# Attention and MLP mixer on one core: the first half of the first queries loaded by GpSimd with a cast, instead of by SyncE and cast on ScalarE

## The chip, the cores and the metric

The kernel runs on one core of a Trainium2 chip. The metric is the time of one execution in microseconds, as the device gives it. Times of several executions are given as a median with the lowest and the highest.

## The reference

Blockwise causal attention, followed by a mixer over tokens and channels. Eight batches, eight heads, 576 tokens, 64 channels per head; all inputs and the output are float32.

```python
scores = scale * np.matmul(q, k.transpose(0, 1, 3, 2))
mask = block_i >= block_j                      # blocks of 64 tokens
scores = np.where(mask, scores, -1000000000.0)
attn = np.exp(scores - np.max(scores, axis=-1, keepdims=True))
attn = attn / (np.sum(attn, axis=-1, keepdims=True) + 1e-09)
x = (attn @ v)                                 # heads side by side: B, 576, 512
h = np.maximum(x.transpose(0, 2, 1) @ w_tok1, 0.0) @ w_tok2
u = x + h.transpose(0, 2, 1)
out = u + np.maximum(u @ w_ch1, 0.0) @ w_ch2
```

## The kernel before

Every piece of work (a load, a cast, a set of matmuls, an evacuation, a store) is an operation with a number. `ORDER` is a written-out list of these numbers, each with the engine that does it (T TensorE, A ScalarE, D VectorE, P GpSimd, S SyncE) and, in small letters, the PSUM banks that it takes. The program is issued in that order, and each engine works through its own share of it strictly in sequence. The order is thus fixed by hand, not by a scheduler at run time, and an operation that waits holds up all that follows on its engine.

A batch goes through these stages: k and q of four heads (a head group, two per batch) are loaded and brought to bf16 in `qk_sb`; VectorE transposes them in blocks of 32 (line 442); TensorE makes the scores of four heads (line 566), ScalarE exponentiates them into `e_sb` (line 585 for batch 0, line 772 for the others); TensorE multiplies with v (`vals`, line 616; line 669 for the last 64 tokens); VectorE normalises into `x_sb`. Then come the token mixer and the channel mixer, whose matmuls fill most of the kernel; the next batches' attention runs between them.

Batch 0 has no work to hide behind, so its loads are cut up. In `load_qk` each of k and q is loaded in two halves of 9 of the 18 rows per partition; q of head group 0 has three pieces, 9, 5 and 4 rows. The first three pieces, both halves of k and the first of q, are loaded by SyncE as float32 into a staging area that lies in `gT` (line 425) and cast to bf16 by VectorE or ScalarE (lines 402 and 400). The other pieces are loaded by GpSimd, which casts on the way (line 437). All loads of v (line 468), of the weights (479, 502, 511) and of later batches' k and q (418) also go through GpSimd's queue. A DMA issued by GpSimd occupies GpSimd while it is issued.

While TensorE has nothing else to do in the first microseconds, it runs matmuls on zeros (lines 371 and 378).

A batch's 512 output rows that this part handles are stored by `channel_down_fast` from the `o_sb` buffers: the upper half (`row == 0`) as one DMA for each 128 rows, the lower half as one DMA for 256 (line 1455). Most stores go through SyncE, where DMA transposes for the channel mixer (lines 969 and 979) stand between them.

Of the kernel before, what the change touches and what calls it, by code (L numbers as in the profile page):

```python
# [27 lines left out]
class Plan:  # L28
# [72 lines left out]
    13S 22P 24P 5P 9D 2D 3P 16S 44Ta 12P 19S 10P 4P 30P 14D 15D 17A 32P 1D 26P 18D 20A 28P 0A 45Tb 23D 25D 21D 252P 46Tb  # L101
    47Tb 48Tb 49Ta 50Ta 37P 51Ta 52Ta 53Ta 54Ta 55Ta 56Ta 35P 57Ta 7D 174Tst 175T 34P 195A 58Ta 59Ta 60Ta
    61Ta 196A 62Ta 38P 197D 63Ta 31D 64Ta 65Ta 66Ta 176A 199Tt 36P 177A 178D 67Ta 179D 68Ta 33D 69Ta 255P 70Ta 200A
    180Ts 27D 198P 71Ta 72Ta 40P 73Ta 181A 29D 182Tt 157P 74Ta 75Ta 76Ta 183A 77Ta 201Ts 43P 78Ta 79Ta 80Ta 253D
    202A 42P 214Tt 254D 188Tb 189T 41P 215A 184Tc 11D 233Ts 6D 190D 191D 258P 192Td 211Ta 234A 220Tt 216P 256D 39P
    185T 257D 221A 81Tb 218Ts 155P 212D 213D 207Tb 235D 208T 186D 219A 158P 187D 237Tt 193D 209D 156P 203Ta 210D
    204T 238A 194D 239Ts 261P 205D 206D 164P 8D 240A 236D 269Tcbda 424P 271A 163P 281Tefgh 270A 166P 259D 273A 217D
    226Tb 283A 227T 284A 222Tc 223T 228D 241Ta 242T 282A 229D 165P 249Tf 224D 245Tg 285A 225D 162P 246T 230Tb 243D
    244D 339Tc 159P 250D 231D 232D 337Ta 251D 247D 161P 340A 260D 272A 276Tbfeh 338D 348Tc 262D 160P 278A 349T 263D
    345Ta 280A 346T 248D 277A 341Td 350D 421P 301Tgbfh 274D 347D 264P 343Tc 342D 303A 275D 351Ta 304A 265P 352T 344D  # L110
    305A 425D 354Td 355T 302A 313Tcbfh 279A 356D 306P 387Tg 353A 267P 426D 384Td 315A 388T 266P 316A 404Ta 385T 317A
    268P 408Tb 314A 381Te 386D 405A 416Tf 427P 409D 390Tc 389A 307P 391T 333D 430P 372Td 392A 308Tabhg 167P 373T
# [12 lines left out]
    553T 623A 763D 543T 620A 547D 676Tg 621A 761D 544A 644Tdehf 542D 926P 677A 554D 555T 647A 764D 560Tag 648A 556D
    561Tc 929P 563A 680Th 557D 765P 562A 684Tf 681D 645A 566T 558T 685D 646A 564Tc 567A 649D 559D 651Tdhef 650P 565A
    768P 638Ta 653A 635Tb 772P 639D 568T 652A 640D 570T 636D 654A 637D 686Ta 569D 655A 656Tbdhe 571D 641Tc 660A 687D
    629Tf 659A 573T 642D 630D 689S 643D 632Ta 658A 631D 682Te 572D 657A 788Tcfdh 633D 634D 574A 673Tb 683D 790A
    670Ta 674D 789A 664Tg 688S 675D 671D 579Tef 672D 791A 665D 792A 666D 769D 783Tbagc 580A 667Td 784A 661Th 668D
    581T 785A 669D 662D 786A 663D 767D 787A 776Tdhba 582D 842Tc 779A 766D 778A 575D 932P 840Tb 780A 941P 770D 777A  # L130
    583Ta 930D 773P 841A 576D 843A 781P 820Tdgeh 939P 577D 585T 771P 821A 578D 824A 775P 584D 694Tbc 850Td 774P 690D
    697A 587T 586D 822A 935P 691D 823A 782P 692D 698Th 851D 848Tg 588D 699A 700T 849D 695Td 701A 704T 696D 702T 589T
    705D 703D 693D 808Tabde 931D 707T 590D 810A 844Tg 812A 846Th 845D 809A 793Tb 591T 708A 847D 811A 794D 795D 813P
    815Tacde 592D 814P 805Tb 1024P 819A 802Tg 594S 806D 818A 799Th 807D 854S 803D 724Tfe 817A 800D 709Tdb 801D 816A
    727D 710Tc 712A 725Th 927D 711A 728Ta 855S 928D 726A 715T 804D 796Tc 729A 934D 730T 716A 713Th 933D 731A 734T
    420S 797D 798D 714A 732T 593S 735D 943Tcgdf 733D 719T 945A 736D 717T 946A 720D 831Ta 944A 834Tg 718D 737T 947A
    722T 835D 836D 738A 828Td 948P 832D 833D 950Tgchf 723A 829D 830D 837Ta 721D 953A 852Tb 838D 952A 839D 857D 825Td
    951A 853D 876Tea 1036P 954A 877Tc 858D 856S 879A 826D 861Tbh 827D 1035P 878A 862Tg 859D 864D 891Tfd 949P 863A
    880Tc 940P 706D 894A 882T 739D 881A 942P 865Tg 897T 937D 866A 938P 867T 936D 883A 884T 860D 1021P 868A 871T 885D
    1030P 869T 898A 886T 872D 1027P 987Tbcef 870D 874T 887D 1034P 990A 895Tg 988A 875D 889T 991A 1007Te 740D 989A  # L140
    896A 890D 955Tbchf 741D 892Ta 959A 899T 1026D 956A 901T 893D 958A 1009Tf 957A 1008D 902D 975Tbach 1010D 972Te
    978A 904T 900D 979A 960Tf 1025D 969Tc 905A 743Tgh 961D 976A 973D 1122P 974D 962D 977A 970D 971D 982Tefdb 980D
    744A 981D 1022D 966Ta 984A 963Tc 1023D 745T 985A 967D 888D 1119P 986A 964D 965D 983A 1037P 995Td 968D 873A 998Tc
    746D 1050Tabfe 1033P 996D 999D 992Tg 1000D 1054A 749T 993D 1053A 994D 997D 1052A 1028D 1038Tcdge 1051A 1029D
    1004Tb 1041A 1031D 1001Ta 1125P 1040A 747Tf 1032D 1039A 1002D 1003D 1128P 1005D 1006D 1082Tdcga 1135P 748D
    1017Tb 1084A 742D 751T 1083A 1018D 1086A 750D 1042A 1045Tcdba 1085A 752D 1043P 753T 1047A 1131P 1121D 757S 1049A
    1120D 1044P 1048A 1077Tdegf 754D 1064Ta 1080A 1124D 1061Tb 755T 1046A 1065D 1062D 1063D 1079A 1078A 1070Tbcge
    1081A 756D 1067Td 1074A 1123D 1058Tf 1073A 1104Th 1066D 1059D 1071A 1060D 1130D 1072A 1055Ta 1143Tfbeg 1105A
    1056D 1075P 1057D 1015Tc 1134P 1068D 1146A 1127D 1013Ta 1145A 1069D 1102Th 1129D 1147A 1076D 1144A 1014D 1093Td
    1103A 1090Tb 1016D 1136Taegf 1126D 1020S 1099Tc 1137A 1094D 1114Th 1091D 1092D 1140A 1100D 1087Ta 1101D 1139A  # L150
    903D 1096Tb 1088D 1112Tc 1138A 1089D 758S 1108Tf 1095D 1115A 1141P 1113D 1106Ta 1132P 1175Tdgeh 1097D 1142D
    1098D 1011Tc 1133P 1107D 1179A 1336Tb 1177A 1012D 1178A 1109D 1168Tachg 1176A 1110Te 1116S 1171A 910Tdf 1170A
    1111D 1337A 1169A 1334Tc 1117S 911D 906D 1148Tbahe 912T 907D 1150A 1019S 1172A 1151A 916T 1173P 913D 1152A 1174P
    1149A 908D 1118S 1180Tadgh 909D 1153Tb 1183A 914Te 1154D 1184A 1155D 1181A 917D 1194Tb 1182A 1335D 1159Tg 1191Th
    1195D 1185Ta 1196D 1197Td 1160D 1192D 1165Tb 1193D 920T 915D 1161D 1198D 1199D 1166D 1188Th 1167D 921D 1162Td
    1156Tb 1189D 1249Tcg 1190D 918T 1163D 1164D 1252A 1200D 1201D 922T 1186D 919D 1157D 1255T 1158D 924S 1279Ted
    1187D 923D 1280Tb 1282A 1350Ta 1256A 1281A 1234Tch 1351A 1344Tf 1237A 1283Tb 1345D 1285T 1284A 1240T 1286A
    1338Ta 1241A 1250Tf 1339D 1253Te 1251A 1287T 1202D 1254A 1348Tc 1288D 1203D 1259T 1349A 1257T 1238Ta 1258D 1289T
    1239A 1235Tb 1290D 1342Tc 1236A 1244T 1291D 1343D 1356Tf 1242T 1245D 1219Tbc 1243D 1360Te 1260D 1220Ta 1361A
    1357D 1262T 1222A 1292T 1364S 1263D 1221A 1340Te 1247T 1293D 1223Ta 1341D 1358Td 1224A 1246D 1204Tfg 1359D 1248A  # L160
    1205Te 1225T 1207D 1206A 1264Tdh 1226A 1229T 1479D 1267A 1265Te 1230D 1208Tb 1266A 1227T 1480D 1209D 1270T
# [1403 lines left out]
```

## Time and profile before

| | |
|---|---|
| median of 3 runs | 284.88 us (284.14 to 289.33) |
| profiled execution | 284.84 us, of it a span of 283.1 us from the first to the last instruction |
| TensorE busy | 276.5 us, 98% of the span |
| VectorE busy | 239.1 us, 84% |
| ScalarE busy | 179.3 us, 63% |
| GpSimd busy | 72.4 us, 26% |
| DMA | 31.97 MB in 64891 packets; software queue (GpSimd) 53.8%, hardware queue (SyncE) 19.7% of 16 engines' time |

In the profile's lines PE is TensorE, PEld its weight loads, DVE VectorE, ACT ScalarE, POOL GpSimd and SPq SyncE's queue. "out<-in" names the tiles written and read; L442 is line 442 of the kernel. The chain is followed back from the last instruction, at each step to what released it.

### The profile page before, as it was taken

The numbers are of one execution on the slowest core, as the hardware profiler recorded it, in microseconds if no ns is written. First come the engines' busy times: TensorE is split into PE (matmuls) and PEld (weight loads), VectorE is DVE, ScalarE is ACT, GpSimd is POOL, SyncE is SP. The second block draws the span as 40 slices with busy tenths as digits, with TensorE's granted clock in tenths as the row PEclk, the third lists the DMA queues.
The fourth block names the chain that finished last, engine by engine and source line by source line (L and its number), as shares of the span: only waits on it lengthen the run. The fifth ranks groups of instructions, "written<-read, shape, count | busy, mean of one in ns | idle before, by whom it ended". The sixth has DMA issues, their size and how long they took to land.

```text
span 283.1 us, 9609 instructions
## 1 busy us (share of the span) xinstructions
PE 276.5 (98%) x4110; PEld 204.7 (72%) x4110; DVE 239.1 (84%) x515; ACT 179.3 (63%) x331; POOL 72.4 (26%) x126
## 2 busy tenths in 40 slices
PE   8999999999999999999999999999999999999995
PEld 3566656588776788986877658756789876568884
DVE  4578669999889898999998979959897897579984
ACT  3798788953998856897779866274533744652200
POOL 8885760511631351063232221000000000000000
PEclk9999999999999999999999999999999999999999
DMA  7999999955989792999698595100044502100157
GB/s 174 161 181 198 198 195 200 140 89 113 109 97 135 81 153 55 165 194 166 72 117 144 43 195 67 59 21 19 0 78 91 206 0 76 74 2 2 74 151 223
DMA packets 64891, 31.97 MB, mean 113 GB/s; under 512 B 53200, under 2 KB 55888, under 8 KB 64848
## 3 DMA queue, kind: packets, MB, share of 16 engines
q0 software_dynamic: 44896, 17.49, 53.8%
q1 hardware_dynamic: 19520, 13.21, 19.7%
q8 instruction: 32, 0.52, 0.8%
q10 hardware_dynamic: 432, 0.66, 0.7%
q14 instruction: 11, 0.09, 0.1%
HBM read 35.85 MB, written 9.44 MB: 160 GB/s over the span
## 4 chain that ended last, share of the span: by engine, by line
PE 90%; POOL 3%; ACT 3%; DMA 2%; issue 1%; DVE 0%; POOLq 0%
PE late L1364 23%; PE mm L1103 8%; PE mm L1230 7%; PE mm L566 7%; PE mm L1364 7%; PE late L1230 6%; PE late L1103 6%; PE mm L616 5%; PE mm L807 3%; PE mm L902 2%; PE late L616 2%; PE late L902 2%; PE late L566 2%; DMA vals<-in_v_dram 2%; PE late L1030 2%; PE mm L1030 2%
## 5 line engine op out<-in xcount | busy, mean ns | idle before, releaser
L772 ACT ACTIVATE e_sb<-mm 128x512 bf16<-128x512 f32 x82 | 46.5, 606 | 13.2 <-PE late L566 9.5
L772 ACT ACTIVATE e_sb<-late 128x512 bf16<-128x512 f32 x86 | 48.4, 609 | 9.2 <-PE late L566 8.4
L442 DVE STREAM_TRANSPOSE qk_sb<-qk_sb 128x288 int32<-128x288 int32 (+1 forms) x65 | 41.7, 693 | 3.8 <-PE late L566 1.8
L468 POOL DMA_DIRECT2D vals<-in_v_dram x45 | 36.9, 832 | 4.7 <-PE mm L616 2.4
L1364 PEld LDWEIGHTS <-gT 128*128 128x128 bf16 x336 | 32.0, 98 | 5.6 <-issue 0.4
L1364 PEld LDWEIGHTS <-sums 128*128 128x128 bf16 x324 | 31.3, 98 | 5.2 <-issue 0.4
L566 PEld LDWEIGHTS <-qk_sb 32*64 32x64 bf16 x1280 | 19.6, 104 | 13.1 <-issue 9.2
L566 PE MATMUL mm<-qk_sb 32*64 32x512 bf16 (+7 forms) x560 | 27.4, 289 | 0.1
L566 PE MATMUL late<-qk_sb 32*64 32x512 bf16 (+7 forms) x560 | 26.8, 295 | 0.6 <-ACT e_sb L585 0.3
L616 PEld LDWEIGHTS <-e_sb 128*128 128x128 bf16 x640 | 23.2, 97 | 5.4 <-issue 2.3
L1364 PE MATMUL late<-wd_sb,gT 128*128 128x256 bf16 x168 | 20.7, 273 | 0.0
L1364 PE MATMUL late<-wd_sb,sums 128*128 128x256 bf16 x168 | 20.6, 273 | 0.0
L1103 PEld LDWEIGHTS <-ws_sb 128*128 128x128 bf16 x192 | 18.2, 98 | 3.0 <-issue 0.9
L616 PE MATMUL mm<-vals,e_sb 128*128 128x65 bf16 x450 | 19.9, 193 | 0.1
L642 DVE TENSOR_TENSOR x_sb<-mm,rinv 128x256 bf16<-128x256 f32 x45 | 18.7, 421 | 1.3
L1410 DVE TENSOR_TENSOR o_sb<-late,u_sb 128x512 f32<-128x512 f32 x22 | 14.9, 683 | 3.6 <-PE late L1364 3.6
L1230 PEld LDWEIGHTS <-ws_sb 128*128 128x128 bf16 x120 | 11.6, 98 | 8.6 <-issue 0.2
L1103 PEld LDWEIGHTS <-wc_sb 128*128 128x128 bf16 x144 | 15.3, 114 | 1.4 <-issue 0.4
L1364 PE MATMUL late<-wc_sb,gT 128*128 128x256 bf16 x132 | 16.2, 272 | 0.0
L594 POOL COPY vals<-e_sb 128x256 bf16<-128x256 bf16 (+1 forms) x11 | 4.3, 392 | 40.6 <-ACT e_sb L772 40.4
L400 ACT COPY mm<-late 128x512 f32<-128x512 f32 (+1 forms) x16 | 9.1, 571 | 8.1 <-PE late L1230 5.3
L793 ACT ACTIVATE gT<-mm 128x512 bf16<-128x512 f32 x21 | 12.6, 616 | 1.9 <-PE mm L1103 0.9
(198 smaller groups left out, 631.8 us busy)
## 6 DMA issues: line engine op xcount, KB each, us to landing
out_dram<-o_sb SPq DMA_DIRECT2D x19, 256.0 KB, 2.4
qk_sb<-in_k_dram POOLq DMA_DIRECT2D x14, 288.0 KB, 6.2
qk_sb<-in_q_dram POOLq DMA_DIRECT2D x14, 288.0 KB, 5.9
vals<-in_v_dram POOLq DMA_DIRECT2D x28, 128.0 KB, 4.8
out_dram<-o_sb SPq DMA_DIRECT2D x7, 512.0 KB, 3.5
wc_sb<-in_moe_w_ch_dram POOLq DMA_DIRECT2D x8, 192.0 KB, 7.0
wc_sb<-in_moe_w_ch_dram POOLq DMA_DIRECT2D x3, 512.0 KB, 10.5
vals<-in_v_dram POOLq DMA_DIRECT2D x15, 64.0 KB, 5.4
```

What stands on the lines that cost most here:

```text
L442: nc.vector.transpose(dst[:, 0:S, :] .rearrange("p s e -> p (s e)") .bitcast(I32) .rearrange("p (a k) -> p k a", k=NB)[:, k0:k1], raw2.bit ...
L468: nc.gpsimd.dma_start(out=t[128 - p : 128, J, hs, 0:64], in_=src)
L566: nc.tensor.matmul(out=home(n)[64 * half : 64 * half + 64, c : c + w], lhsT=bar[r, 0] if j is None else kT[i][r, 64 * j : 64 * j + 64, par ...
L616: nc.tensor.matmul(out=u[:, I, 0:65], lhsT=e[:, h, c : c + 128], rhs=vt[:, J, head, 0:65], start=(J == 0), stop=(J == I),)
L642: nc.vector.tensor_tensor(out=xt[:, 0:4, 64 * head : 64 * head + 64], in0=u[:, :, 0:64], in1=ri[:, 0:4].to_broadcast([128, 4, 64]), op=MULT,)
L772: nc.scalar.activation(dst, bank_of(x), EXP, scale=scale)
L793: nc.scalar.activation(dst, src, RELU)
L902: nc.tensor.matmul(out=bank_of(bank), lhsT=w2_sb[:, t, 128 * si : 128 * si + 128], rhs=at[:, t, :], start=(t == 0), stop=(t == NDT - 1),)
L1103: nc.tensor.matmul(out=bank_of(bank)[:, 256 * o_ : 256 * o_ + 256], lhsT=x(o_, m), rhs=y[:, :, m, :], start=opens, stop=m == 1, skip_group ...
L1230: nc.tensor.matmul(out=bank_of(bank)[:, 128 * c : 128 * (c + step)], lhsT=x(m), rhs=y[:, c : c + step, m, :], start=opens, stop=m == 1, sk ...
L1364: nc.tensor.matmul(out=bank_of(bank)[:, 256 * i : 256 * i + 256], lhsT=x[:, kk, 128 * i : 128 * i + 128], rhs=y[:, kk], start=first and i ...
L1410: nc.vector.tensor_tensor(out=dst, in0=src, in1=other, op=ADD)
```

## The change

The first piece of q of batch 0, head group 0 (9 of 18 rows) is no longer loaded by SyncE into the staging area and cast on ScalarE; it is loaded by GpSimd, cast on the way, as the first DMA of GpSimd's queue. Its transpose on VectorE now comes first of the three of q instead of last. One operation falls away, so all later numbers in `ORDER` go down by one; the sequence of the others on every engine is unchanged. And the store of the lower half of batch 0's rows goes out as two DMAs of 128 rows instead of one of 256. It is the first of the stores that SyncE issues at 118.60 us.

```diff
 ORDER = """
-    13S 22P 24P 5P 9D 2D 3P 16S 44Ta 12P 19S 10P 4P 30P 14D 15D 17A 32P 1D 26P 18D 20A 28P 0A 45Tb 23D 25D 21D 252P 46Tb
+    13S 19P 21P 23P 5P 9D 2D 3P 16S 43Ta 12P 10P 4P 29P 14D 15D 17A 31P 1D 25P 18D 27P 0A 44Tb 20D 22D 24D 251P 45Tb
...
-                if first and not hg and n + f < 2:
+                if first and not hg and n == 0:
                     def emit_load(o, k0=k0, k1=k1, hbm=hbm, n=n):
                         nc.sync.dma_start(out=stage[n][:, D * k0 : D * k1], in_=hbm[:, D * k0 : D * k1])
...
                 def emit(o, row=row, cols=slice(256 * h0, 256 * h1), c0=c0, nt=nt):
-                    step = 1 if row == 0 else nt
+                    step = 1 if row == 0 or b == 0 else nt
                     for t0 in range(c0, c0 + nt, step):
```

In the upper line of `ORDER`, 19S, 20A and 21D are the load, the cast and the transpose of the piece in question, 22P to 25D loads and transposes of the other two pieces of q. In the lower line 19P and 20D are its load and transpose.

More of the change, by code (lines that the diff above doesn't have):

```diff
@@ L176 @@
[L176 to L178 removed]
+    13S 19P 21P 23P 5P 9D 2D 3P 16S 43Ta 12P 10P 4P 29P 14D 15D 17A 31P 1D 25P 18D 27P 0A 44Tb 20D 22D 24D 251P 45Tb
+    46Tb 47Tb 48Ta 49Ta 36P 50Ta 51Ta 52Ta 53Ta 54Ta 55Ta 34P 56Ta 7D 173Tst 174T 33P 194A 57Ta 58Ta 59Ta 60Ta 195A 61Ta
@@ new lines @@
+    240Ta 241T 281A 228D 164P 248Tf 223D 244Tg 284A 224D 161P 245T 229Tb 242D 243D 338Tc 158P 249D 230D 231D 336Ta 250D
+    246D 160P 339A 259D 271A 275Tbfeh 337D 347Tc 261D 159P 277A 348T 262D 344Ta 279A 345T 247D 276A 340Td 349D 420P
+    300Tgbfh 273D 346D 263P 342Tc 341D 302A 274D 350Ta 303A 264P 351T 343D 304A 424D 353Td 354T 301A 312Tcbfh 278A 355D
+    305P 386Tg 352A 266P 425D 383Td 314A 387T 265P 315A 403Ta 384T 316A 267P 407Tb 313A 380Te 385D 404A 415Tf 426P 408D
+    389Tc 388A 306P 390T 332D 429P 371Td 391A 307Tabhg 166P 372T 310A 333D 381T 167P 309A 368Tc 308A 369T 168P 416A
@@ new lines @@
+    1052A 993D 996D 1051A 1027D 1037Tcdge 1050A 1028D 1003Tb 1040A 1030D 1000Ta 1124P 1039A 746Tf 1031D 1038A 1001D
+    1002D 1127P 1004D 1005D 1081Tdcga 1134P 747D 1016Tb 1083A 741D 750T 1082A 1017D 1085A 749D 1041A 1044Tcdba 1084A
+    751D 1042P 752T 1046A 1130P 1120D 756S 1048A 1119D 1043P 1047A 1076Tdegf 753D 1063Ta 1079A 1123D 1060Tb 754T 1045A
+    1064D 1061D 1062D 1078A 1077A 1069Tbcge 1080A 755D 1066Td 1073A 1122D 1057Tf 1072A 1103Th 1065D 1058D 1070A 1059D
+    1129D 1071A 1054Ta 1142Tfbeg 1104A 1055D 1074P 1056D 1014Tc 1133P 1067D 1145A 1126D 1012Ta 1144A 1068D 1101Th 1128D
@@ new lines @@
+    1146A 1075D 1143A 1013D 1092Td 1102A 1089Tb 1015D 1135Taegf 1125D 1019S 1098Tc 1136A 1093D 1113Th 1090D 1091D 1139A
+    1099D 1086Ta 1100D 1138A 902D 1095Tb 1087D 1111Tc 1137A 1088D 757S 1107Tf 1094D 1114A 1140P 1112D 1105Ta 1131P
+    1174Tdgeh 1096D 1141D 1097D 1010Tc 1132P 1106D 1178A 1335Tb 1176A 1011D 1177A 1108D 1167Tachg 1175A 1109Te 1115S
+    1170A 909Tdf 1169A 1110D 1336A 1168A 1333Tc 1116S 910D 905D 1147Tbahe 911T 906D 1149A 1018S 1171A 1150A 915T 1172P
+    912D 1151A 1173P 1148A 907D 1117S 1179Tadgh 908D 1152Tb 1182A 913Te 1153D 1183A 1154D 1180A 916D 1193Tb 1181A 1334D
@@ new lines @@
+    1442A 1328D 1384Te 1386A 1402Td 1399Tc 1385A 1329T 1403A 1400A 1408T 1330D 1406T 1389T 1332S 1407D 1368Tcg 1390A
+    1443Tef 1409D 1371A 1387Td 1411T 1388A 1374T 1412D 1446A 1372Ta 1393T 1524D 1373A 1375D 1369Th 1449T 1394D 1370A
+    1447Tc 1425D 1391T 1448A 1444Th 1392D 1450A 1378T 1445A 1453T 1494D 1379D 1451T 1395A 1376T 1454D 1381T 1396T 1456T
+    1397A 1531Tde 1457D 1382A 1458D 1462Tbh 1459D 1466Tg 1460D 1463A 1461D 1468T 1532D 1527D 1464T 1467D 1535Tf 1465D
+    1452D 1470T 1528D 1455A 1469D 1537T 1529D 1377D 1472T 1471D 1380A 1410D 1476S 1533T 1530D 1473D 1573Tbc 1569D
```

130 lines of the change are left out of this document (53 added, 77 removed).

## The prediction

> **What bounds the kernel now.** I read the page first (busy shares, then the chain that ended last), then the chain in order of time for the first 45 us, because the change acts there.
>
> ```profile
> span 283.1 us, 9609 instructions
> PE 276.5 (98%) x4110; PEld 204.7 (72%) x4110; DVE 239.1 (84%) x515; ACT 179.3 (63%) x331; POOL 72.4 (26%) x126
> PE 90%; POOL 3%; ACT 3%; DMA 2%; issue 1%; DVE 0%; POOLq 0%
> ```
>
> TensorE is busy for 98% of the span and holds 90% of the chain. The other tenth lies at the start. In order of time the chain there reads:
>
> ```profile
> 1.26 1.24 POOL qk_sb L437 x2
> ...
> 6.92 2.78 POOL vals L468 x4
> 9.70 5.39 DMA vals<-in_v_dram
> ...
> 15.13 0.40 PE mm L616 x8
> 15.53 0.63 PE sc L566 x14
> ...
> 16.18 4.99 ACT e_sb L585 x5
> ...
> 21.22 0.66 PE late L566 x14
> ```
>
> The columns are start, length and what ran. The chain does not pass through the first scores. It passes down GpSimd's queue: two q loads, the small fills, six more q and k loads, four v loads, then the fifth v load issued at 9.70, which lands 5.39 later. That landing lets TensorE do value products at 15.13, the scores queued behind them at 15.53, and so ScalarE's exponentials from 16.18. From there ScalarE sets the pace for 4.99 us, and then TensorE. The view by windows says what follows leaves nothing to catch up with:
>
> ```profile
> 22.00:60.00 38.00, 37.39 (x703) 24.37 (x703) 31.90 (x74) 32.81 (x67) 19.16 (x32) 1.00 1.32 184
> 60.00:120.00 60.00, 60.00 (x1087) 48.08 (x1084) 55.56 (x128) 44.03 (x87) 17.45 (x29) 1.00 0.93 107
> ```
>
> The first number in front of a bracket is TensorE's busy time: 37.39 of 38, then 60 of 60. A microsecond gained or lost at 16.18 is one at the end.
>
> **What feeds the first scores.** They wait for five transposes on VectorE, two of k and three of q (timeline, start and length; a bracket is the wait before):
>
> ```profile
> 1.66 0.43 SPq L425 DMA_DIRECT2D gT<-in_q_dram  x1
> 4.47 0.72 DVE L442 STREAM_TRANSPOSE qk_sb<-qk_sb 128x288 int32<-128x288 int32 x1
> 5.19 0.71 DVE L442 STREAM_TRANSPOSE qk_sb<-qk_sb 128x288 int32<-128x288 int32 x1
> 6.37 1.59 DVE L442 STREAM_TRANSPOSE qk_sb<-qk_sb 128x160 int32<-128x160 int32 x3 [0.47 <-DMA qk_sb<-in_q_dram]
> 6.55 0.67 ACT L400 CAST qk_sb<-gT 128x576 bf16<-128x576 f32 x1 [1.39 <-DMA gT<-in_q_dram]
> 8.02 0.51 PE L566 MATMUL sc<-qk_sb 32*64 32x192 bf16 x28 [0.60 <-DVE qk_sb L442]
> 8.78 7.13 ACT L585 ACTIVATE e_sb<-sc 128x384 bf16<-128x384 f32 x9 [1.45 <-PE sc L566]
> 16.18 4.98 ACT L585 ACTIVATE e_sb<-sc 128x1024 bf16<-128x1024 f32 x5 [0.28 <-PE sc L566]
> ```
>
> VectorE is free from 5.90 and waits until 6.37 for GpSimd's first q load; the three q transposes end at 7.96 and the scores start at 8.02. Nine exponentials run from 8.78 to 15.91, then ScalarE idles 0.28 us for the scores that the v load held back. An earlier first exponential therefore only lengthens that 0.28.
>
> **Part 1: what goes.** The cast of 0.67 us stands on ScalarE between idle times of 1.39 and 1.45 us, so its removal is worth 0. SyncE's third issue, 0.43 us, has nothing behind it on SyncE until a store at 66: 0.
>
> **Part 2: the added issue on GpSimd.** The load of the q half goes to the head of GpSimd's queue, ahead of everything that the chain passes through.
>
> ```profile
> L437 POOL DMA_DIRECT2D qk_sb<-in_q_dram x4: 538/550/689, 1.3 to 4.8; - x4
> DMA to landing us min/median/max: 4.1/4.7/5.1
> 4.24 1.08 POOL L437 DMA_DIRECT2D qk_sb<-in_q_dram  x2
> 5.31 1.08 POOL L437 DMA_DIRECT2D qk_sb<-in_k_dram  x2
> 6.35 0.57 POOL L418 DMA_DIRECT2D qk_sb<-in_k_dram  x1
> 6.87 3.65 POOL L468 DMA_DIRECT2D vals<-in_v_dram  x5
> ```
>
> An issue of this kind holds GpSimd 0.54 to 0.69 us, 0.55 in the middle. GpSimd never waits between 1.26 and the end of these rows, so nothing swallows it: all of the queue moves by 0.55, two q loads, the fills, four loads of the second head group, one of the next batch, five of v. The fifth v issue goes from 9.70 to 10.25.
>
> **Part 3: does the landing move as much as the issue?** At most it moves by the issue (0.69 for the longest). At least by 0, if the DMA engines have a backlog that the issue only joins later. The windows of half a microsecond decide (second-last column: share of the DMA engines; last: GB/s):
>
> ```profile
> 5.00:5.50 0.50, 0.50 (x3) 0.20 (x2) 0.50 (x3) 0.15 (x1) 0.50 (x2) 1.00 0.83 153
> 5.50:6.00 0.50, 0.50 (x4) 0.24 (x3) 0.40 (x1) 0.00 (x0) 0.50 (x2) 1.00 0.95 87
> 6.00:6.50 0.50, 0.50 (x7) 0.45 (x6) 0.13 (x1) 0.00 (x0) 0.50 (x2) 1.00 0.95 151
> 6.50:7.00 0.50, 0.50 (x7) 0.46 (x5) 0.50 (x2) 0.45 (x1) 0.50 (x2) 1.00 1.16 175
> ```
>
> From 6.5 on the engines are more than full, so there is a backlog. But between 5 and 6.5 they are not, and move as little as 87 GB/s: the first group's q is nearly in, and the second group's loads, issued from 4.24, have hardly begun. In the new kernel these are issued from 4.79, while the bytes of the first group are the same, so that thin stretch grows and the backlog behind it starts later, by nearly the whole 0.55. I take 0.5 of 0 to 0.69. Behind the fifth v landing (15.09) everything moves by 0.5: ScalarE's second run from 16.18 to 16.68. The last v load of that batch lands near 22 on the same queue and has the same shift, so it is not added.
>
> **Part 4: the first scores.** The new load is first in GpSimd's queue and takes the 4.1 to 5.1 us of the rows of its kind. They hold at most its own size, 144 KB as landed, so I take the upper one, which the first load of the queue had:
>
> ```profile
> gT<-in_q_dram SPq DMA_DIRECT2D x1, 288.0 KB, 4.9
> qk_sb<-in_q_dram POOLq DMA_DIRECT2D x1, 80.0 KB, 5.1
> qk_sb<-in_q_dram POOLq DMA_DIRECT2D x1, 64.0 KB, 4.8
> ```
>
> 1.26 + 5.1 = 6.36, and the transposes, now in the order of the loads, run 6.36 to 7.95 if the other two pieces (issued 1.81 and 2.36) land by 7.1 and 7.5; 2.36 + 4.8 = 7.16 does. So the first scores start as before: 0. The wait for this piece now stands ahead of the other two q transposes on VectorE; TensorE's first scores wait for all three either way, so only the last end counts. Early end: all land 4.1 after issue, VectorE starts at 5.90 and ends at 7.49, 0.47 earlier, which lengthens ScalarE's idle and brings nothing. Late end: a landing of 6.6 us, the longest beside these, among all loads of q and k in the first 20 us:
>
> ```profile
> DMA to landing us min/median/max: 4.1/5.1/6.6
> ```
>
> 1.26 + 6.6 = 7.86, so 1.49 later; that is the second rival.
>
> The fit of the Trainium skill for a load by GpSimd (DMA: Bandwidth & Descriptors, Anatomy of one DMA — SWDGE (gpsimd) path: about 2.0 us plus the bytes at 436 GB/s) would give 2.7 us for the 288 KB read, an estimate by that page; all three pieces would be in before 5.90, which is the early end, with the same end time. The trace has 4.8 to 5.1 us for smaller pieces, so here the measurement decides against it.
>
> **Part 5: the split store.** Batch 0's lower rows leave SyncE as two stores, after two transposes by DMA:
>
> ```profile
> 111.36 0.41 SPq L1455 DMA_DIRECT2D out_dram<-o_sb  x1
> 118.60 2.19 SPq L1455 DMA_DIRECT2D out_dram<-o_sb  x3
> 122.96 1.20 SPq L979 DMA_TRANSPOSE umT<-um_sb  x1
> ```
>
> One more issue costs 0.41. The stores end at 120.79 and the next transpose, which waits for its data, starts at 122.96: 2.17 us cover it. Without that cover it would be 0.41 on the transposed mean rows, whose readers lie far off the chain. 0.
>
> **Sum.** 0 + 0 + 0.5 + 0 + 0 = +0.5 us. The profiled execution took 284.84 us (span 283.1 and 1.74 around it), which is the median of the runs, 284.88, to within 0.04. So 284.84 + 0.5 = 285.3 us.
>
> **The rivals.**
> 1. *The shift is swallowed; not slower.* The backlog after 6.5 us hides the later issue, the v loads land at 15.09 as before. For it: the shares above 1. Against it: the thin stretch just before. Price 0, and if the v data even gain a little from an emptier hardware queue, at most ScalarE's 0.28: 284.6 to 284.8.
> 2. *The q half lands late; slower.* The place is VectorE's first q transpose, now waiting for a longer load through GpSimd. It decides once the nine exponentials, ending at 15.91 plus its delay, end after 16.68, a delay of 0.77, that is a landing 5.9 us after issue. At 6.6 us the delay is 1.49, the exponentials end at 17.40, 1.22 later than 16.18: 286.1. For it: this piece is 1.8 times the longest of the first two. Against it: loads of 144 KB took 4.1 to 5.1.
> 3. *TensorE slows down in the pause; slower.* The trace shows two speeds of the same idle-filling matmuls:
>
> ```profile
> 1.20 4.80 PE L371 MATMUL mm<-wd_sb 128*128 128x512 bf16 x11 [1.20 <-DVE wd_sb L344]
> 5.83 1.58 PE L378 MATMUL mm<-wd_sb 128*128 128x256 bf16 x13
> ```
>
> 0.436 us for 512 columns at first, 0.122 for 256 later, 1.8 times slower per column. The pause before the first scores, 0.60 now, would be 2.1 in the late case, and one before 15.13 grows to about 0.7. If such a pause brings the slow speed back for as long as at the start (4.6 us), it costs 4.6 x (1 - 1/1.8) = 2.0: 287.4. For it: the speed plainly depends on what went before. Against it: the pause of 0.60 did no harm, and filler matmuls stand behind it. By the Trainium skill (TensorE: Matmul & The Clock Gate, Part 1) the array falls back only after an idle window of about 3.4 us, which neither pause reaches; no run here shows that limit.
>
> **How the numbers follow.** Chances: forecast 0.55; first rival 0.22; second 0.13; third 0.06; 0.04 for what I don't see. The runs shown reach from 284.14 to 289.33, so a difference under 2% (5.7 us) can hardly be told from none; all named cases lie inside it. The range goes from 284.0 (the first rival less the 0.7 between the median and the lowest run) to 287.0 (the second with as much on top). Over 2%: only what I don't see, or the third twice, and runs like 289.33: faster 0.05, slower 0.10, within 0.85.
>
> **What would show it.** Right: GpSimd's queue 0.5 to 0.6 later from the fills on; the fifth v issue at about 10.25 and its landing near 15.6; ScalarE's wait before the second run of exponentials up from 0.28 to near 0.8; first exponential within 0.5 of 8.78; no cast on ScalarE after 5.2; TensorE as full as before from 22. Wrong: the v landing at 15.1 or earlier (first rival), VectorE's q transposes starting after 7.2 (second), filler matmuls of 256 columns 0.2 us apart after 8 us (third), or a new gap at 118 to 125 from the split store.

## The result and the profile after

The changed kernel took 288.46 us in the median of 22 executions (284.54 to 291.16), the kernel before 285.3 us in the median of 22 beside it (284.14 to 289.33). The ratio is 1.0063 with a 95% interval of 1.0033 to 1.0092; it leaves out executions more than 1.5% above the fastest of their kernel, which the medians hold, so it is smaller than the medians' ratio. The forecast was 285.3 us with a range up to 287.0: the sign of the shift was right, its size and its cause were not.

The profiled execution of the changed kernel took 289.64 us. From its page, the span, the busy shares, the granted clock of TensorE in 40 slices (7.2 us each), and the chain's shares:

```profile
span 287.8 us, 9588 instructions
PE 279.2 (97%) x4089; PEld 207.9 (72%) x4110; DVE 239.3 (83%) x515; ACT 178.7 (62%) x330; POOL 73.1 (25%) x127
PEclk9955999999999999999999999999999999999999
PE 91%; POOL 3%; DMA 2%; ACT 1%; issue 1%; DVE 0%; POOLq 0%
```

In the page of before the same clock line is 9 throughout:

```profile
PEclk9999999999999999999999999999999999999999
```

The chain still ends on TensorE and still begins in GpSimd's queue, so the list of shares tells almost nothing. The two fives do: from the third slice TensorE ran at half its clock. The windows of one microsecond say exactly when (columns as in the prediction; the first number is TensorE's busy time, the third from the end its granted clock):

```profile
5.00:6.00 1.00, 1.00 (x8) 0.70 (x7) 0.99 (x2) 0.08 (x1) 0.98 (x3) 1.00 0.35 44
6.00:7.00 1.00, 1.00 (x18) 0.71 (x15) 0.89 (x4) 0.00 (x0) 1.00 (x3) 1.00 0.61 54
...
14.00:15.00 1.00, 0.00 (x0) 0.00 (x0) 0.99 (x4) 0.87 (x1) 0.72 (x2) 1.00 1.32 161
15.00:16.00 1.00, 0.41 (x5) 0.35 (x6) 0.04 (x1) 0.00 (x0) 0.34 (x1) 0.64 1.60 188
16.00:17.00 1.00, 0.94 (x19) 0.77 (x21) 0.39 (x2) 0.00 (x0) 1.00 (x2) 0.50 1.24 166
...
28.00:29.00 1.00, 1.00 (x24) 0.84 (x22) 0.93 (x5) 0.92 (x2) 0.20 (x1) 0.54 1.16 206
29.00:30.00 1.00, 1.00 (x30) 0.91 (x27) 0.56 (x5) 0.00 (x0) 0.55 (x2) 1.00 1.14 210
```

TensorE stands still through the whole of 14 to 15, the clock falls inside 15 to 16 (0.64 of it is left, so at 15.3 to 15.4), and is back at about 28.9: 13.6 us at half speed. The first two rows belong to another point: from 5 to 7 the DMA engines are busy for only 0.35 and 0.61 of the time and move 44 and 54 GB/s.

The timeline of the same execution shows why TensorE stood still and what the half clock cost (start, length, what; a bracket is the idle time before it):

```profile
5.01 1.80 DVE L439 STREAM_TRANSPOSE qk_sb<-qk_sb 128x288 int32<-128x288 int32 x4
6.97 0.51 PE L563 MATMUL sc<-qk_sb 32*64 32x192 bf16 x28
7.71 3.65 POOL L465 DMA_DIRECT2D vals<-in_v_dram  x5
7.74 7.13 ACT L582 ACTIVATE e_sb<-sc 128x384 bf16<-128x384 f32 x9 [2.66 <-PE sc L563]
13.19 0.59 PE L563 MATMUL sc<-qk_sb 32*64 32x256 bf16 x18
15.59 1.11 PE L613 MATMUL mm<-vals,e_sb 128*128 128x65 bf16 x13 [1.82 <-DMA vals<-in_v_dram]
17.77 1.02 ACT L582 ACTIVATE e_sb<-sc 128x1024 bf16<-128x1024 f32 x1 [2.90 <-PE sc L563]
19.43 1.02 ACT L582 ACTIVATE e_sb<-sc 128x1024 bf16<-128x1024 f32 x1 [0.64 <-PE sc L563]
...
24.44 1.02 ACT L582 ACTIVATE e_sb<-sc 128x1024 bf16<-128x1024 f32 x1 [0.65 <-PE sc L563]
```

Two things move apart. The first scores start at 6.97 instead of 8.02 and the first exponentials at 7.74 instead of 8.78: TensorE runs out of work 1.05 us sooner. The v loads go out at 7.71 instead of 6.87, and the fifth lands later:

```profile
5.26 1.96 POOL qk_sb L434 x4
7.75 2.77 POOL vals L465 x4
10.53 5.54 DMA vals<-in_v_dram
16.11 0.60 PE mm L613 x8
16.70 0.95 PE sc L563 x13
```

That is the chain in order of time: landing at 16.07, where it was 15.09 before. The products that need the earlier v loads start at 15.59, where they started at 14.74 with no wait ahead of them:

```profile
14.74 0.79 PE L616 MATMUL mm<-vals,e_sb 128*128 128x65 bf16 x13
```

So the pause of 1.82 us is the sum of two shifts, 1.05 from the scores and 0.85 from v, less a little. The clock falls within it, and the loss can be read off ScalarE. Before, its second run of five exponentials was one row without a gap, 16.18 to 21.16. Now the first starts at 17.77 and each of the other four waits 0.63 to 0.67 us for scores made at half clock, up to 25.46. That is 4.3 us later, of the 4.7 by which the span grew: 0.98 because the eight products that the fifth landing lets go start later (16.11 for 15.13), 0.61 because they and the scores behind them run at half clock (1.66 until 17.77, where it was 1.05), 2.6 in the four gaps, and 0.1 of rounding. So about 1 us of the loss is lateness, and 3.2 us go by at half clock.

The clock does not fall in every execution. By mean granted clock the 22 executions fall into two groups: 18 at 0.976 to 0.982 with a median of 288.82 us, and 4 at 0.998 to 1.00 with a median of 284.67. I call these "fell" (a mean clock below 0.99) and "held". The kernel before does it too, but seldom: of its 126 executions beside the experiments 20 fell (median 288.3) and 106 held (median 285.02). What the change did is to turn a fall in 16 of 100 executions into one in 82 of 100.

### The profile page after: what moved, and what is told of

It reads as the page before. It is cut to its first block, busy times and chain, and to the rows that moved or that the text cites. A ratio compares the mean times of both kernels' runs of the same rounds, so it can differ in the third digit from the quotient of the medians.

```text
span 287.8 us, 9588 instructions
## 1 busy us (share of the span) xinstructions
PE 279.2 (97%) x4089; PEld 207.9 (72%) x4110; DVE 239.3 (83%) x515; ACT 178.7 (62%) x330; POOL 73.1 (25%) x127
## 4 chain that ended last, share of the span: by engine, by line
PE 91%; POOL 3%; DMA 2%; ACT 1%; issue 1%; DVE 0%; POOLq 0%
PE late L1361 23%; PE mm L1100 7%; PE mm L1227 7%; PE mm L1361 7%; PE mm L563 7%; PE late L1227 6%; PE mm L613 6%; PE late L1100 6%; PE mm L804 2%; PE late L613 2%; PE late L563 2%; DMA vals<-in_v_dram 2%; PE late L899 2%; PE mm L666 2%; PE mm L899 2%; PE late L1027 2%
## 5 line engine op out<-in xcount | busy, mean ns | idle before, releaser
L563 PEld LDWEIGHTS <-qk_sb 32*64 32x64 bf16 x1280 | 20.8, 108 | 13.5 <-issue 9.6
L613 PEld LDWEIGHTS <-e_sb 128*128 128x128 bf16 x640 | 24.8, 101 | 7.4 <-issue 3.5
L613 PE MATMUL mm<-vals,e_sb 128*128 128x65 bf16 x450 | 21.6, 201 | 1.9 <-DMA vals<-in_v_dram 1.8
L582 ACT ACTIVATE e_sb<-sc 128x1024 bf16<-128x1024 f32 (+2 forms) x14 | 12.2, 906 | 8.2 <-PE sc L563 8.1
L1100 PEld LDWEIGHTS <-wc_sb 128*128 128x128 bf16 x144 | 15.3, 114 | 1.4 <-issue 0.4
L633 DVE RECIPROCAL rinv<-mm 128x4 f32<-128x4 f32 x45 | 7.5, 171 | 10.0 <-PE mm L613 10.0
```

Source lines behind the costliest of these rows:

```text
L563: nc.tensor.matmul(out=home(n)[64 * half : 64 * half + 64, c : c + w], lhsT=bar[r, 0] if j is None else kT[i][r, 64 * j : 64 * j + 64, par ...
L582: nc.scalar.activation(dst, sc[SC.index(note["pool"])][:, :, cols], EXP, scale=scale)
L613: nc.tensor.matmul(out=u[:, I, 0:65], lhsT=e[:, h, c : c + 128], rhs=vt[:, J, head, 0:65], start=(J == 0), stop=(J == I),)
L1100: nc.tensor.matmul(out=bank_of(bank)[:, 256 * o_ : 256 * o_ + 256], lhsT=x(o_, m), rhs=y[:, :, m, :], start=opens, stop=m == 1, skip_group ...
```

## The experiments

Theory A: TensorE idle time ahead of the first value products makes the granted clock fall, and the change lengthened that idle time from two sides (earlier scores, later v). Rivals: B, the split store or another part of the change costs the time; C, the later landing of v is itself the loss, and the clock only goes along with it; D, GpSimd's load at the head of the queue costs of itself. Each kernel ran 10 to 12 times unless a smaller number is given. The expectations were written before the runs.

**The load alone.** The changed kernel with the store as before:

```diff
-                    step = 1 if row == 0 or b == 0 else nt
+                    step = 1 if row == 0 else nt
```

> The moved load without the split store. Theory A (TensorE's pause of 1.8 us before the first value products halves its clock for 10 to 14 us): the same as the changed kernel, most runs 287.5 to 289.5 us with a mean granted clock of 0.976 to 0.982, a few at 284.5 to 285 with 1.00. Theory B (the split store costs it): all runs near 285, clock 1.00.

Measured: 288.78 us, ratio 1.0073 [1.0028, 1.0118]; 8 of 12 fell (289.2), 4 held (285.23). The load alone reproduces the loss, and its profile has the wait for v:

```profile
15.66 0.41 PE L613 MATMUL mm<-vals,e_sb 128*128 128x65 bf16 x5 [1.31 <-DMA vals<-in_v_dram]
```

**The store alone.** The kernel before with `or b == 0` added in that line.

> The kernel before with the split store alone. Theory A: as the kernel before, 284.2 to 286 us in most runs, ratio 0.998 to 1.002. Theory B: 1.5 to 3 us more than the kernel before.

Measured: 286.29 us, ratio 1.0022 [0.999, 1.0053], 2 of 12 fell. The store costs nothing that can be told from zero (the interval ends at 0.53%, 1.5 us), and the load alone has the whole loss, so B is out as its cause. Its profiled execution was an odd one, and useful. A k load landed late, 5.39 us after its issue, TensorE paused for 2.37 us, and the clock held:

```profile
9.17 0.51 PE L566 MATMUL sc<-qk_sb 32*64 32x192 bf16 x28 [2.37 <-DVE qk_sb L442]
```

A shorter lull of the same execution, near 23, brought a fall:

```profile
8.00:9.00 1.00, 0.00 (x0) 0.10 (x1) 1.00 (x4) 0.18 (x2) 0.66 (x2) 1.00 1.06 179
...
22.00:23.00 1.00, 0.66 (x15) 0.15 (x15) 0.00 (x0) 1.00 (x3) 0.51 (x1) 1.00 1.53 190
23.00:24.00 1.00, 0.06 (x1) 0.00 (x0) 0.00 (x0) 1.00 (x3) 0.00 (x0) 1.00 1.39 181
24.00:25.00 1.00, 0.77 (x10) 0.33 (x9) 0.83 (x2) 1.00 (x4) 0.73 (x2) 1.00 1.03 189
25.00:26.00 1.00, 0.96 (x18) 0.96 (x19) 0.58 (x3) 0.64 (x2) 0.53 (x2) 0.51 1.13 199
```

Some 1.5 us of idle time in 22 to 25, then half clock from 25.0, for 3.5 us. (Its mean clock of 0.993 puts this execution under "held".) The length of the pause alone does not decide.

**Fill the pause.** The changed kernel with 16 more filler matmuls ahead of the first value products (187Tb):

```diff
-... 41P 213Tt 253D 187Tb
+... 41P 213Tt 253D 81Ta 82Ta 83Ta ... 96Ta 187Tb
```

> The changed kernel with 16 more idle-filling matmuls of 256 columns (16 x 0.11 = 1.8 us) in front of the first value products, where TensorE pauses 1.82 us for v; everything else as it was. Theory A: the granted clock stays at 1.00 in nearly all runs and the time falls to 284.5 to 285.2 us. Theory C (v's later landing itself is the loss, and the clock only follows): 287 to 289 us as before, whatever the clock.

Measured: 287.42 us, ratio 1.0081 [1.0043, 1.0119], but 0 of 10 fell. The clock was cured and the time was not: the fillers take longer than the wait that they fill.

```profile
14.75 1.92 PE L375 MATMUL mm<-wd_sb 128*128 128x256 bf16 x16
16.51 0.55 PE L613 MATMUL mm<-vals,e_sb 128*128 128x65 bf16 x13
```

The products start at 16.51 with no wait for v. By the number alone it is theory C that was met, and A's 284.5 to 285.2 was missed; but the time is now that of the fillers, so this run does not part the two.

**Half as many.** The same with 8 fillers (81Ta to 88Ta).

> The changed kernel with 8 more idle-filling matmuls in front of the first value products, half of what e3_fill_pause put in: 0.9 us of work, which leaves about 0.9 us of the 1.82 us pause and lies inside the wait for v. Theory A (the pause halves the clock, and e3 was slow because its 1.8 us of filling outlasted the wait): clock 1.00 in nearly all runs and 284.5 to 285.5 us in most. Theory C (v's later landing itself is the loss): 286.5 to 289 us even at a clock of 1.00.

Measured: 285.36 us, ratio 1.0016 [0.9999, 1.0033], 0 of 11 fell.

```profile
13.58 1.05 PE L375 MATMUL mm<-wd_sb 128*128 128x256 bf16 x8
15.06 0.33 PE L613 MATMUL mm<-vals,e_sb 128*128 128x65 bf16 x5 [0.44 <-DMA vals<-in_v_dram]
15.69 0.40 PE L613 MATMUL mm<-vals,e_sb 128*128 128x65 bf16 x8 [0.30 <-DMA vals<-in_v_dram]
```

No load is moved, the products still wait for v, and about 3 us are back. In this profile the eight products start at 15.69, 0.42 us sooner than in the changed kernel's, far less than the time won. What is left, 0.16% or 0.45 us, is what the forecast had for the whole change. Against C.

**A quarter.** Four fillers (81Ta to 84Ta), to find how much idle time the clock bears.

> The changed kernel with 4 more idle-filling matmuls in front of the first value products: the pause of 1.82 us becomes about 1.3 to 1.4. A threshold between the pauses that left the clock alone (0.4 to 0.9 us) and those that halved it (1.43 and 1.82 us) is looked for. If what counts is how much of a fixed stretch of about 3.4 us TensorE is idle, with the limit near 1.4 us: clock 1.00 in most runs, below 0.985 in up to a third; 285 to 286 us in the good ones. If any pause above 1 us does it: below 0.985 in two thirds, 287.5 to 289.5 us.

Measured: 285.59 us, ratio 1.0009 [0.9976, 1.0042], 1 of 12 fell. In its profile a wait of 0.98 us is left and the clock holds:

```profile
15.62 0.79 PE L613 MATMUL mm<-vals,e_sb 128*128 128x65 bf16 x13 [0.98 <-DMA vals<-in_v_dram]
```

**A late v in the kernel before.** Nothing of the change; only one of GpSimd's loads (a first q load of the next batch) is put ahead of the v loads:

```diff
-... 252P 46Tb
+... 252P 255P 46Tb
...
-... 69Ta 255P 70Ta
+... 69Ta 70Ta
```

> The kernel before, SyncE's load of the q half in place, with a load of the next batch's q (288 KB as landed) issued ahead of the v loads instead of behind them: v lands 1.5 to 2 us later. Theory A: a pause of 1.5 to 2 us in front of the first value products although the moved load is not there, clock 0.976 to 0.982 in more than half of the runs, which then take 287.5 to 290 us. Theory D (it is something else about the moved load, its cast by DMA or VectorE's order): clock 1.00 as in the kernel before, 1 to 2 us more at most.

Measured: 289.78 us, ratio 1.0161 [1.0135, 1.0187], and 5 of 5 fell. The v loads go out at 8.30 instead of 6.87; TensorE waits 1.43 us, and the clock halves as in the changed kernel:

```profile
15.76 0.33 PE L616 MATMUL mm<-vals,e_sb 128*128 128x65 bf16 x5 [1.43 <-DMA vals<-in_v_dram]
```

Without the moved q load the loss is there, so D is out: a late v is enough. It doesn't part A from C, since here v is late too.

**Idle time with nothing late.** The kernel before without the 23 fillers between the first sets of scores; no load is moved:

```diff
-... 195A 58Ta 59Ta 60Ta ... 78Ta 79Ta 80Ta ...
+... 195A ...
```

> The kernel before without the 23 filler matmuls that stand between the first sets of scores (operations 58Ta to 80Tb). No load, cast or other operation is moved, so nothing lands later; TensorE only has about 3.4 us more of idle time, spread in pieces over 8.7 to 14 us. Theory A (idle TensorE time of itself halves the granted clock, whatever caused it): the clock falls to 0.5 for one stretch or several in most executions, mean clock about 0.97 to 0.985, 287.5 to 290 us. Theory C (the loss comes from the later landing of v, the clock only goes along with it): no landing moves, 284.5 to 285.3. Between the two, if the idle time is in pieces too short: 285, with the clock at 1.00.

Measured: 289.02 us, ratio 1.0101 [1.0055, 1.0148], 6 of 6 fell (mean clock 0.97 to 0.976).

```profile
9.48 0.38 PE L566 MATMUL sc<-qk_sb 32*64 32x448 bf16 x2 [1.17 <-ACT e_sb L585]
10.46 0.39 PE L566 MATMUL sc<-qk_sb 32*64 32x448 bf16 x2 [0.34 <-ACT e_sb L585]
11.38 0.64 PE L566 MATMUL sc<-qk_sb 32*64 32x512 bf16 x8 [0.27 <-ACT e_sb L585]
12.29 0.76 PE L566 MATMUL sc<-qk_sb 32*64 32x512 bf16 x8 [0.27 <-ACT e_sb L585]
14.20 1.09 PE L616 MATMUL mm<-vals,e_sb 128*128 128x65 bf16 x13
```

and its windows:

```profile
11.00:12.00 1.00, 0.73 (x18) 0.14 (x8) 1.00 (x3) 1.00 (x2) 0.96 (x3) 1.00 1.49 162
12.00:13.00 1.00, 0.73 (x11) 0.14 (x8) 0.09 (x1) 1.00 (x2) 0.47 (x2) 0.84 2.33 163
13.00:14.00 1.00, 0.84 (x25) 0.75 (x21) 0.91 (x2) 1.00 (x2) 1.00 (x3) 0.50 1.88 136
...
26.00:27.00 1.00, 1.00 (x30) 0.91 (x28) 0.93 (x4) 1.00 (x4) 0.65 (x2) 0.83 1.13 204
```

The value products wait for no v and start at 14.20, earlier than in the kernel before; nothing else is late. The clock falls at 12.7, before any of them, and returns at 26.3. So idle time alone makes the clock fall, here in pieces of 0.27 to 1.17 us. With the eight fillers above, which bring the time back though v comes late, that decides for A against C as the cause of most of the loss.

**An idle pause before the first scores.** The kernel before without nine early fillers (49Ta to 57Ta).

> The kernel before without 9 of the 13 idle-filling matmuls ahead of the first scores: no load, no transpose and no wait is moved, only TensorE pauses 1.7 us there instead of 0.60. Theory A: the clock falls in more than a third of the runs to 0.976 to 0.99, and these take 2 to 4.5 us more. Theory C (lateness, not the pause): no change, ratio 0.999 to 1.001, since nothing is later.

Measured: 284.78 us, ratio 0.9996 [0.9964, 1.0028], 1 of 12 fell and 3 more showed 0.994. In its profile the first scores started at 7.42 and the pause was 0.49 us, so the case wanted was not made; it decides nothing.

**Take the lateness away.** The changed kernel with the second head group's four loads ahead of GpSimd's small fills, so that the v loads no longer queue behind both (a call further down moves with them, so that these loads no longer depend on the fills):

```diff
-    13S 19P 21P 23P 5P 9D 2D 3P 16S 43Ta 12P 10P 4P 29P 14D 15D 17A 31P 1D 25P 18D 27P 0A ...
+    13S 19P 21P 23P 29P 31P 25P 27P 5P 9D 2D 3P 16S 43Ta 12P 10P 4P 14D 15D 17A 1D 18D 0A ...
```

> The changed kernel with the second head group's four loads ahead of GpSimd's small fills, so that the DMA engines do not run dry between 5.2 and 6.4 us. Theory A: v lands up to 1 us earlier, the pause falls from 1.82 to 0.6 to 1.2 us, the clock stays at 1.00 in most runs; 284.0 to 284.8 us in these. If the dry stretch does not set v's landing (GpSimd's issue does): the pause stays at 1.8 us and the times at 287.5 to 289.5.

Measured: 285.03 us, ratio 0.9974 [0.994, 1.0008]; 4 of 12 fell, 8 held (284.44). In the profiled execution TensorE does not wait for v, and ScalarE's second run starts half a microsecond earlier than before the change. Why 4 of 12 fell all the same, this profile, of one that held, does not show:

```profile
15.70 4.98 ACT L582 ACTIVATE e_sb<-sc 128x1024 bf16<-128x1024 f32 x5 [0.38 <-PE sc L563]
```

**The same order in the kernel before.**

> The kernel before with the second head group's loads ahead of GpSimd's fills, as in e4_fills_later, the q half still loaded by SyncE. Against e4 it shows what the moved load is worth once v comes early enough. If the moved load's earlier first scores count: e4's good runs (284.2 to 284.8) are 0.3 to 1 us below this one's. If they do not: equal within 0.3 us.

Measured: 284.88 us, ratio 1.0006 [0.9985, 1.0026], 0 of 12 fell. The order of the loads brings nothing measurable by itself. No execution fell; with 16 falls in 100, as in the kernel before, that comes up by chance about once in eight times. The held executions of the reordered changed kernel (284.44) are 0.44 us below this run's, which by the expectation says that its earlier first scores count; with 8 and 12 executions spread over 1.2 and 2.2 us that is a hint and no more.

**Order and fillers.** The reordered changed kernel with six fillers ahead of the value products, and with three there and three before the scores 173Tst:

> The order of e4_fills_later with 6 idle-filling matmuls (0.65 us) in front of the first value products. Theory A: the third of e4's runs that fell to 0.976 to 0.982 no longer does; all near 284.2 to 285.2 us, faster than the kernel before by 0.2 to 0.4% in the mean. Theory C: slower than e4 by the 0.65 us in its good runs, as many bad ones.

> The order of e4_fills_later with 3 idle-filling matmuls (0.33 us) in front of the first scores and 3 in front of the first value products. Theory A: e4's falls of the clock (4 of 12 runs) come from these two pauses and go; 284.2 to 285.2 us in all runs, 0.1 to 0.4% below the kernel before. Otherwise as e7_fills_later_some_fill, 285 to 286.5 us.

Measured: 285.92 us, 1.0034 [1.0009, 1.0059], and 285.82 us, 1.0037 [1.0004, 1.007]; 1 of 12 fell in each. Both expectations had these faster than the kernel before; they are slower. One fall of 12 instead of 4 may be the fillers' doing, and they pay more than they get: held executions are at 285.88 and 285.71, against 284.44 without fillers.

**Fillers in the kernel before.** Eight (82Ta to 89Ta) ahead of 188Tb.

> The kernel before with the 8 idle-filling matmuls of e5_half_fill in front of the first value products, where it has hardly a pause (0.16 us). The price of the filling itself: 0.4 to 0.9 us more than the kernel before, clock 1.00 in all runs. If e5's recovery came from something other than the filled pause, this one would gain too.

Measured: 286.2 us, ratio 1.0029 [1.0001, 1.0057], 0 of 12 fell. Where TensorE has no wait to fill, eight fillers cost about 1.2 us against the held 285.02. That none fell is, as above, no proof that they take away the falls.

**Shorten the pause without filling it.** The five v loads in another order, the rows that the first products read first:

```diff
-... 36P ... 34P ... 33P ... 37P ... 35P
+... 34P ... 33P ... 35P ... 36P ... 37P
```

In the changed kernel:

> The changed kernel with the five first loads of v in another order: the rows that the first value products read are issued first, so that the products can start before the fifth load lands. No filler is added. Theory A: the pause ahead of the first value products becomes shorter than 1.4 us and the clock stays at 1.00 in most executions; about 284.3 to 285.2 us. Rival (the load of the q half costs of itself, by its place in the queue): 285.5 to 288.8 as in the changed kernel. If the products need the last rows anyway, the order is worth nothing and the median is near 288.5.

Measured: 286.04 us, ratio 0.9981 [0.9937, 1.0024]; 3 of 12 fell. Better than the changed kernel's 18 of 22, yet the nine that held have a median of 285.46 with a wide spread, up to 286.99. In the profiled one, that of 286.99 at full clock, TensorE is idle in places where it was busy before:

```profile
22.00:23.00 1.00, 0.45 (x10) 0.33 (x10) 0.83 (x2) 1.00 (x3) 0.77 (x2) 1.00 1.43 161
...
28.00:29.00 1.00, 0.16 (x1) 0.10 (x1) 0.63 (x2) 0.27 (x1) 0.00 (x0) 1.00 1.13 207
```

That part I can't explain.

In the changed kernel together with the order of the q and k loads:

> The changed kernel with the second head group's q and k loads ahead of GpSimd's fills, and the new order of the v loads as well. Theory A: the pause is shortened by the earlier queue and by the order, both without filler; the clock stays at 1.00 in all or nearly all executions, and the earlier first scores reach the end: 284.0 to 284.6 us, the lowest of all. Rival (only fillers keep the clock): it falls in 4 of 12 or more as with the earlier queue alone.

Measured: 284.79 us (284.26 to 289.42), ratio 0.9975 [0.9945, 1.0005], just above the expected 284.0 to 284.6; 1 of 12 fell. The profiled execution was that one:

```profile
15.63 0.62 PE L613 MATMUL mm<-vals,e_sb 128*128 128x65 bf16 x8 [1.31 <-DMA vals<-in_v_dram]
```

The five products that read the early rows no longer wait; the eight behind them do, for 1.31 us, and the clock falls all the same. And in the kernel before, v order alone:

> The kernel before with the new order of the v loads alone. ScalarE waits only 0.28 us for scores held up by the v load, and the first scores stay at 8.0, so at most 0.3 us can be gained: 284.6 to 285.3, clock 1.00 as before. If it gains more, the order of v and not the moved q load is what counts in the combination.

Measured: 284.55 us, ratio 0.9982 [0.9947, 1.0017]; 1 of 12 fell. ScalarE's wait of 0.28 us is gone, its 14 exponentials run through:

```profile
9.05 12.16 ACT L585 ACTIVATE e_sb<-sc 128x384 bf16<-128x384 f32 x14 [1.46 <-PE sc L566]
```

The last two have lower medians than both kernels, by 0.6 and 0.8 us against the 285.37 beside them, but both intervals hold 1. That the moved q load is worth anything in the combination isn't shown: 284.79 with it, 284.55 without.

| | runs | fell | held median | all median |
|---|---|---|---|---|
| before, beside the experiments | 126 | 20 | 285.02 | 285.3 in the 22 beside the changed kernel |
| changed | 22 | 18 | 284.67 | 288.46 |
| load alone | 12 | 8 | 285.23 | 288.78 |
| changed, 4 / 8 / 16 fillers | 12 / 11 / 10 | 1 / 0 / 0 | 285.39 / 285.36 / 287.42 | 285.59 / 285.36 / 287.42 |
| changed, order of loads | 12 | 4 | 284.44 | 285.03 |
| changed, order of loads and of v | 12 | 1 | 284.78 | 284.79 |
| before, late v | 5 | 5 | none | 289.78 |
| before, 23 fillers fewer | 6 | 6 | none | 289.02 |

## Why the prediction was wrong, point by point

**Part 1 (what goes): half right.** ScalarE idles 2.66 us before the first exponentials, so the cast was worth nothing to ScalarE. But it also stood on the way to the first scores. Before, it ended at 7.22 (6.55 and 0.67), and the last transpose of q, which reads it, started at 7.25. While it stood there, earlier landings of the other two pieces could not have brought the scores forward.

**Part 5 (the store): right.** The store alone gave 1.0022 with 1 inside the interval. SyncE's row of stores grew by more than the 0.41 taken (3.09 us for four, 2.19 for three), but it still ends 2.4 us before the next transpose.

**Part 2 (the issue): right, and in this execution short.** The queue moved by 0.84 us at the v loads (6.87 to 7.71), not 0.55. One issue more makes 0.53 (1.77 for three against 1.24 for two); the other 0.3 is GpSimd's fill of `ident`, 0.51 us where it was 0.20:

```profile
3.72 0.51 POOL masks.py:197 MEMSET ident<- 128x128 bf16 x1
```

In the changed order it can meet VectorE's cast of k (3.58 to 4.09). There are six profiled executions with the load at the head of the queue and the fills where they were (the changed kernel, load alone, 4, 8 and 16 fillers, v order). In three of them the cast starts 0.11 to 0.14 us ahead of the fill, which takes 0.51; in the other three the two start within 0.02 us of each other, and the fill takes 0.20. The v loads of these six start at 7.48 to 7.71, against 6.87 to 7.17 in five with SyncE's load (before, fewer early fillers, 23 fewer, eight fillers, v order; the store alone, with its late k load, is left out). Between the middles, 7.60 and 7.13, lies about the half microsecond forecast.

**Part 3 (the landing): the row was the right one, read too low.** The thin stretch of the DMA engines grew as said, down to 44 GB/s in 5 to 6. The landing moved by 0.98, more than the issue's 0.84, not 0.5. Whether +0.5 us at the end is real where the clock holds stays open: with eight fillers it was 0.45 us with 1 just inside the interval, while the held executions of the changed kernel and of the load alone, eight together, have a median of 285.07 against 285.02, and none of them was profiled.

**Part 4 (the first scores): wrong, and the first step that failed.** I took the upper price, 5.1 us, for the landing of the new load, "which the first load of the queue had", and got 0 with 0.47 as the early end. It landed in 3.7 us and the others in 3.5 and 3.3, beyond the early end, which had 4.1. The view of DMA issues, first 3 us (size as landed, us to landing):

```profile
qk_sb<-in_q_dram POOLq DMA_DIRECT2D x1, 144.0 KB, 3.7
qk_sb<-in_q_dram POOLq DMA_DIRECT2D x1, 80.0 KB, 3.5
qk_sb<-in_q_dram POOLq DMA_DIRECT2D x1, 64.0 KB, 3.3
```

The rows of 4.8 to 5.1 came from a time in which three loads of SyncE, 288 KB each as landed, shared the DMA engines with GpSimd's two. The change took one of the three away; the same rows of q now come through GpSimd's own queue, 144 KB as landed. I priced the load that came and left out what the load that went had cost its neighbours. VectorE ran its transposes without a wait from 5.01, so the scores came 1.05 us earlier. One pair of profiles overstates it: in the six executions named above the first exponential starts at 7.60 to 8.79 (middle 8.02), in the five at 8.19 to 9.05 (middle 8.70). The gain is some 0.7 us, and the landings of the two pieces that were GpSimd's before are 3.3 to 3.9 us in the six and 3.5 to 5.3 in the five. That the missing load is what made them faster fits these rows and was not tried by itself. The estimate that the Trainium skill's fit gave (DMA: Bandwidth & Descriptors, Anatomy of one DMA — SWDGE (gpsimd) path), 2.7 us, lies on the other side: the measured 3.7 is a little nearer to it (1.0) than to my 5.1 (1.4).

I also wrote that an early end "brings nothing" because it only lengthens ScalarE's idle time. That is the deeper error. An earlier start of one engine is only free if the idle time it makes does no harm, and on TensorE it did.

**Rival 3 (TensorE slows down in the pause): it is what happened, at 0.06.** The mechanism was the right one, with three wrong sizes. Its pause ahead of the v products was put at about 0.7 us, because Part 4 held the scores in place (and with some 0.2 of a pause already there, where TensorE had no wait before 14.74); it was 1.82 in the changed kernel's profile and 1.31 in that of the load alone. Its price was put at 2.0 us, from 4.6 us at 1/1.8 speed, which was the slow start of the kernel; the clock was at half for 13.6 us and cost 4.15 (288.82 - 284.67). The granted clock reads 1.00 in that slow start, so the record does not show that the two are the same thing. And its chance was low because the pause of 0.60 did no harm, which was no evidence on pauses of another length.

I leant there on a rule. By the Trainium skill (TensorE: Matmul & The Clock Gate, Part 1: The HAM clock gate) the clock is set by free-running windows of about 3.4 us and falls after one that was idle. The stretches here fit windows of that length: most executions below 0.997 show mean clocks of 0.994, 0.982, 0.976 and 0.970, that is one, three, four and five times 3.4 us at half of a span of 283 (0.006 each). That a whole window must be idle does not fit: pauses of 1.43 and 1.82 us, and pieces of 0.27 to 1.17, were followed by a fall, while one of 2.37 was not. A free-running window that falls when enough of it is idle could explain both, as a pause then counts by where it lies. In the execution with the pause of 2.37 us (6.80 to 9.17), steps of 3.41 us back from its fall at 25.0 put a boundary at 7.95, and the two windows hold 1.15 and 1.31 us of idle time. But the 3.41 us ahead of a fall hold 1.51 (changed), 1.59 (store alone), 1.42 (late v) and 1.10 (23 fillers fewer), so no one limit parts falls from holds in these rows. The rule stays open.

**Rivals 1 and 2** did not come: v landed later, not at 15.09, and the q half landed early, not late.

**The range.** 284.0 to 287.0 holds the four held executions and not the median. It left out rival 3 for its chance alone; a case with a known mechanism and a price of several microseconds belongs inside it.

## What to carry to other kernels

Price a load that leaves a queue by what shares the DMA engines with it, not by its own issue alone: two q loads that the edit did not touch landed up to 1.6 us faster, though that cause was not tried by itself. When an engine is going to start sooner, follow it to its next wait, and add the time by which that wait's releaser comes later: two shifts of about a microsecond opened a pause of 1.82 us. And where TensorE carries the end, look at the granted clock behind every pause of about a microsecond, and behind several shorter ones close together, in several executions, before calling idle time free. Fillers kept the clock here, but they cost time as soon as they outlast the wait that they fill.

## What the runs showed of the hardware that I had not expected

TensorE's granted clock fell to half in 5 of 5 executions of a kernel whose profile shows a pause of 1.43 us, and in 18 of 22 with the change, whose profile shows 1.82 us, and it stayed there for 10 to 14 us, though TensorE had work nearly all that time. With 0.98 us left in the profile 1 of 12 fell. Since the same program falls in one execution and holds in the next, a kernel near that edge has two times 3 to 4 us apart (3.3 before, 4.15 with the change), and a change of a microsecond in a load moves the share between them. Why the slow stretch lasts one window of 3.4 us in a few executions and three to five in most, with TensorE busy nearly throughout, no run explains.

A fill of 128x128 on GpSimd took 0.51 us instead of 0.20 in the three executions in which VectorE's cast had started 0.11 to 0.14 us ahead of it. The Trainium skill (SBUF — State Buffer, SBUF: two separate sides) says that VectorE and GpSimd share a port pair that one holds for a whole instruction; these three agree, with the fill ending at 4.23 and the cast at 4.09. In the three in which both started within 0.02 us the fill took 0.20 beside the cast, and which of them came first can't be read.
